# Linear attention and two feed-forward layers on one core: two attention units in one visit, a state kept twice, scores computed a visit ahead

## The chip, the cores and the metric

The kernel runs on one core of a Trainium2 chip. The metric is the device time of one execution, in microseconds (us). Five engines matter: TensorE (PE in the profile, its weight loads are PEld), VectorE (DVE), ScalarE (ACT), GpSimd (POOL), and SyncE (SP), which here does nothing but issue DMAs. Each engine runs its own instructions in the order of the program and waits on semaphores for the others.

## The reference: what is computed

A recurrent attention with a decay w for each feature and a bonus u, then two feed-forward layers. B = 4 batches, H = 8 heads, S = 768 tokens, D = 48.

```python
for t in range(S):
    cur = einsum('bhd,bhe->bhde', u[None] * k_t, v_t)
    y[:, :, t] = einsum('bhd,bhde->bhe', r_t, state + cur)
    state = w[None, :, :, None] * state + einsum('bhd,bhe->bhde', k_t, v_t)
x = y as (3072 tokens, 384)
h = x @ w_in;  g = max(h, 0) + alpha * min(h, 0);  x = g @ w_out       # first layer, 384 -> 2048 -> 384
h = x @ w_in2; g = h * tanh(softplus(h));          out = g @ w_out2    # second layer, same sizes
```

## The kernel before

The 768 tokens are cut into six blocks of 128 tokens; with four batches a block has 512 columns. **The first feed-forward layer** (stage A) is a row of 96 slots, one for each pair of a block and one of 16 hidden tiles of 128 features. A slot is nine TensorE matmuls of 128x512 into a PSUM tile `h` (`mA_h`, line 269: x and w are split into a high and a low part, which takes three passes), the activation on ScalarE and VectorE (`mA_g`: `m` on line 673, `g` on line 675), a split of g into `ghi` (`mA_hi`, line 187, ScalarE) and `glo` (`mA_lo`, line 190, VectorE), and nine matmuls into accumulators `acc` (`mA_out`, line 705), which run two slots later (`LAG`). Tile `h` has two buffers. **The second layer** (stage B) follows with 96 slots of its own and is not touched.

**The attention** feeds x to stage A block by block. It is worked in units. Units 0 to 3 are the first block, one batch each. From unit 4 on, a unit is a block j, a pair of batches bp and a half of 64 tokens (`seat_of_unit`): 4 units to a block, 24 in all. The order in a block before is pair 0 first half, pair 0 second half, pair 1 first half, pair 1 second half. A unit's small matmuls stand between two slots, after a slot's h matmuls and before its out matmuls: I call that a **visit**. `batch(u)` makes it: eight matmuls of the state with r for the other batch of the row group (`carried(False)`, line 534), the scores of unit u+1 (line 501), the products of k and v that update the state (line 550, `more_state`), the eight other carried matmuls (line 534), and masked scores times v (line 557). The profile shows each of these float32 matmuls as two records, 128 records to a full visit. The result stands in a `yt` bank and in one of the two buffers of `h`.

Around it, for each unit: the state T is multiplied in place by w to the 64th (`t_decay`, line 566 on ScalarE or 568 on VectorE; `other()` says which engine is free in a phase), the update is added (`t_update`, line 574, VectorE), `x_parts(u)` splits the result into the parts of x (ScalarE line 187, four operations with output y or x, then VectorE line 190, four). Since a head has 48 features, the last two heads fit into free rows of x, so x_parts of a second half also issues six DMAs on SyncE that move them there (line 639, `x<-y`). Ahead of a unit stand its loads (`load_unit`: r and k through line 301 for a pair's first half, `nat` through line 324), the scaling of r and k (`prep_pair`, line 419), the bonus terms (`prep_c`, `prep_c2`, `prep_kn`), the diagonal (`preset`, into tile `Ah`) and the mask (`masked`, line 505, VectorE, from the PSUM tile `sc` into `Ah`).

The order of all of this is a plan: `at(place, work)` puts a piece of work at a place counted in slots, a table `PLACES` overrides places of the first slots, and `run_plan` sorts by place. In `plan_unit(u, s)` the visit of unit u stands at s + 0.60, `t_decay` at s + 0.61, `x_parts` at s + 0.70, `t_update` at s + 1.25, and s comes from `AT`: every fourth slot from unit 6 on.

Of the kernel before, what the change touches and what calls it, by code (L numbers as in the profile page):

```python
# [31 lines left out]
C = 128  # L32
# [5 lines left out]
PR = 112  # L38
# [10 lines left out]
def seat_of_unit(u):  # L49

    j, r = divmod(u, 4)
    return j, r // 2, r % 2


def more_state(u):
# [10 lines left out]
    "pad_v 0": 8.499, "m_first 1": 8.549, "keep_warm 3##########": 8.599, "scores 0": 8.649, "dma_start": 8.699,  # L66
    "seats": 8.749, "masked 0": 8.799, "c_first 1": 8.849, "load_unit 3": 8.899, "prep_rk 1": 8.949,
    "load_unit 2": 8.999, "m_first 2": 9.049, "scale_Kn": 9.099, "more_raw 3": 9.149, "pad_v 1": 9.199,
# [20 lines left out]
    "mA_g 1": 14.049, "half_tables": 14.099, "states_first 0": 14.149, "w_hi (0,3)": 14.199, "w_lo (0,3)": 14.249,  # L89
# [74 lines left out]
def attention_and_two_ff(ctx: ExitStack, tc, rkT, nat, wT, ub, consts, w1, w2, alphaT, out):  # L164
# [353 lines left out]

    def batch(u):

        j, bp, half = seat_of_unit(u)
        pair, n, v = inp[u]
        A = A_t.pop(u)
        y = yt_t[u] = [bank("yt"), bank("h", 2)]
# [16 lines left out]
        if u + 1 < NU:  # L541
            scores(u + 1)
# [592 lines left out]
```

## Time and profile before

| | |
|---|---|
| device time, median of 3 runs | 860.72 us (860.19 to 861.66) |
| the profiled execution's own time, and its span | 860.91 us, 859.2 us |
| TensorE busy | 853.1 us, 99% of the span, granted clock full in every slice |
| VectorE, ScalarE, GpSimd busy | 629.2 us, 617.5 us, 109.3 us |
| chain that ended last | 95% of it is TensorE |

The span is the time between the first and the last instruction that the profiler recorded; the run's own time is 1.7 us longer. A busy TensorE counts a matmul from the start of its stream to its modelled end, so small matmuls that lie behind each other still show as busy.

### The profile page before, as it was taken

The numbers are of one execution on the slowest core, as the hardware profiler recorded it, in microseconds if no ns is written. First come the engines' busy times: TensorE is split into PE (matmuls) and PEld (weight loads), VectorE is DVE, ScalarE is ACT, GpSimd is POOL, SyncE is SP. The second block draws the span as 40 slices with busy tenths as digits, with TensorE's granted clock in tenths as the row PEclk, the third lists the DMA queues.
The fourth block names the chain that finished last, engine by engine and source line by source line (L and its number), as shares of the span: only waits on it lengthen the run. The fifth ranks groups of instructions, "written<-read, shape, count | busy, mean of one in ns | idle before, by whom it ended". The sixth has DMA issues, their size and how long they took to land.

```text
span 859.2 us, 16705 instructions
## 1 busy us (share of the span) xinstructions
PE 853.1 (99%) x6380; PEld 709.6 (83%) x6380; DVE 629.2 (73%) x974; ACT 617.5 (72%) x1205; POOL 109.3 (13%) x127
## 2 busy tenths in 40 slices
PE   9999999999999999999999999999999999999998
PEld 6888788888888888888888888888888888888897
DVE  8888666566656656554766878887887887887876
ACT  5989464445445445544656989989999998998886
POOL 3555441112211112100002000000000000000000
PEclk9999999999999999999999999999999999999999
DMA  9986644354255434213520200110110110100101
GB/s 335 283 260 176 184 144 130 90 194 137 86 161 167 145 98 158 65 65 134 161 87 6 111 1 2 32 43 1 29 46 1 28 47 0 28 11 1 26 12 37
DMA packets 65328, 79.95 MB, mean 93 GB/s; under 512 B 39648, under 2 KB 52448, under 8 KB 65248
## 3 DMA queue, kind: packets, MB, share of 16 engines
q1 hardware_dynamic: 64688, 78.78, 30.0%
q8 instruction: 50, 0.82, 0.4%
q14 instruction: 30, 0.25, 0.1%
q10 hardware_dynamic: 560, 0.10, 0.1%
HBM read 61.16 MB, written 15.73 MB: 89 GB/s over the span
## 4 chain that ended last, share of the span: by engine, by line
PE 95%; DMA 2%; ACT 2%; SPq 1%; DVE 0%; issue 0%; POOL 0%; ACTq 0%; DVEq 0%; POOLq 0%
PE h L269 45%; PE acc L705 22%; PE sc L835 8%; PE acc L835 8%; PE yt L835 4%; PE acc L833 3%; PE sc L501 1%; PE yt L833 1%; DMA w4r<-in_w 1%; PE h L534 1%; PE yt L557 1%; PE sc L550 1%; PE yt L534 1%; DMA w8u<-in_rkT 0%; SPq L639 0%
## 5 line engine op out<-in xcount | busy, mean ns | idle before, releaser
L269 PE MATMUL h<-x,w 128*128 128x512 f32 (+1 forms) x1746 | 415.3, 388 | 0.0
L269 PEld LDWEIGHTS h<-x,w 128*128 128x128 f32 x1746 | 325.3, 188 | 67.0 <-issue 0.4
L705 PE MATMUL acc<-ghi,w 128*128 128x512 f32 x516 | 174.9, 394 | 0.0
L673 ACT ACTIVATE m<-h 128x512 f32<-128x512 f32 x96 | 57.1, 595 | 91.1 <-PE h L269 90.9
L675 DVE SCALAR_TENSOR_TENSOR g<-m,oma,h 128x512 f32<-128x512 f32 x96 | 71.6, 746 | 60.7 <-ACT m L673 59.5
L705 PEld LDWEIGHTS acc<-ghi,w 128*128 128x128 f32 x516 | 96.9, 188 | 21.2
L187 ACT ACTIVATE ghi<-g 128x512 fp32r<-128x512 f32 x86 | 54.1, 630 | 68.9 <-PE acc L705 46.3
L705 PE MATMUL acc<-glo,w 128*128 128x512 f32 x258 | 100.5, 390 | 0.0
L190 DVE TENSOR_TENSOR glo<-g,ghi 128x512 fp32r<-128x512 f32 x86 | 62.4, 726 | 50.7 <-ACT ghi L187 50.2
L771 DVE SCALAR_TENSOR_TENSOR a<-ghi,h 128x512 f32<-128x512 f32 x96 | 66.0, 688 | 37.7 <-ACT ghi L768 31.2
L771 DVE SCALAR_TENSOR_TENSOR g<-s,c 128x512 f32<-128x512 f32 x95 | 66.6, 702 | 22.6 <-ACT s L768 21.0
L779 ACT ACTIVATE m<-h 128x512 f32<-128x512 f32 x96 | 56.4, 588 | 35.0 <-PE h L269 35.0
L190 DVE TENSOR_TENSOR gloB<-g,ghiB 128x512 fp32r<-128x512 f32 x105 | 72.1, 686 | 6.7 <-ACT ghiB L187 6.7
L768 ACT ACTIVATE ghi<-m,biases 128x512 f32<-128x512 f32 x96 | 69.6, 725 | 3.2
L187 ACT ACTIVATE ghiB<-g 128x512 fp32r<-128x512 f32 x105 | 64.8, 617 | 9.1 <-PE acc L705 5.5
L768 ACT ACTIVATE glo<-ghi,biases 128x512 f32<-128x512 f32 x96 | 68.1, 710 | 0.1
L768 ACT ACTIVATE s<-glo,biases 128x512 f32<-128x512 f32 x96 | 68.1, 709 | 0.0
L768 ACT ACTIVATE s<-s,biases 128x512 f32<-128x512 f32 x96 | 68.0, 708 | 0.0
L835 PE MATMUL sc<-ghiB,w 128*128 128x512 f32 x192 | 66.9, 389 | 0.0
L771 DVE SCALAR_TENSOR_TENSOR b<-ghi,a 128x512 f32<-128x512 f32 x96 | 65.7, 684 | 0.1
L771 DVE SCALAR_TENSOR_TENSOR c<-glo,b 128x512 f32<-128x512 f32 x95 | 65.7, 691 | 0.0
L835 PE MATMUL acc<-ghiB,w 128*128 128x512 f32 x192 | 61.7, 389 | 0.0
(200 smaller groups left out, 1149.9 us busy)
## 6 DMA issues: line engine op xcount, KB each, us to landing
wrawr<-in_w SPq DMA_DIRECT2D x28, 768.0 KB, 5.8
nat<-in_nat SPq DMA_DIRECT2D x40, 288.0 KB, 4.4
w2d<-wj SPq DMA_DIRECT2D x16, 384.0 KB, 2.6
wraw<-w2d SPq DMA_DIRECT2D x16, 384.0 KB, 3.0
rk<-in_rkT SPq DMA_DIRECT2D x40, 128.0 KB, 2.8
x2d<-xo SPq DMA_DIRECT2D x6, 768.0 KB, 3.8
x<-x2d SPq DMA_DIRECT2D x6, 768.0 KB, 4.4
rk<-in_rkT SPq DMA_DIRECT2D x40, 96.0 KB, 2.6
```

The lines of the kernel that those rows point to most:

```text
L187: act.activation(out=hi, in_=src, func=AF.Copy)
L190: eng.tensor_tensor(out=lo, in0=src, in1=hi.bitcast(F32), op=ALU.subtract)
L269: pe.matmul(h[:, n], w_in(layer, f, a, c), x[:, b, c, n], start=(k == 0), stop=(k == 3 * KC - 1))
L534: pe.matmul((y if same else over)[i][64 * q:64 * q + 64, p * HC:(p + 1) * HC], T[ROWS[h], 2 * bp + i, k, :], pair[i][ROWS[h], 0, k, t], st ...
L673: act.activation(out=m, in_=hA[s], func=AF.Relu, scale=-1.0)
L675: dve.scalar_tensor_tensor(out=g, in0=m, scalar=oma[:, f:f + 1], in1=hA.pop(s), op0=ALU.mult, op1=ALU.add)
L705: pe.matmul(acc[0][c], w_out(0, f, a)[:, c * 128:(c + 1) * 128], g[b], start=(f == 0 and k == 0), stop=(f == NF - 1 and k == 2))
L768: act.activation(out=out, in_=in_, func=AF.Square, scale=scale, bias=fin[bias])
L771: dve.scalar_tensor_tensor(out=out, in0=in0, scalar=scalar, in1=in1, op0=op0, op1=ALU.mult)
L779: act.activation(out=bnew("t", n), in_=v["h", n], func=AF.Tanh, scale=0.5)
L833: pe.matmul(acc[1][t][:, :DM], g[a][:, t * C:(t + 1) * C], w_out(1, f, b), **se)
L835: pe.matmul(acc[1][t], w_out(1, f, a)[:, t * 128:(t + 1) * 128], g[b], **se)
```

## The change: what it does

From block 2 on (the third), units 8 to 23, **two units share one visit**: `two(a)` handles units a and a+1, which are now both batch pairs of one half (`seat_of_unit` swaps the order for j of 2 or more). Eight visits stand at the slots of `AT2`, seven slots apart. Before the first of them a small visit of its own, `scores_of_two(8)`, computes the scores of units 8 and 9; from then on a visit ends with the scores of the next two units. The state has two tiles, T and Tn: `fade` on ScalarE writes the decayed state from the one to the other a good slot behind a visit, and in the next visit VectorE adds the products of k and v to it (line 722) as soon as the states matmuls are there; carried goes on reading the old tile. r and k of a block come in one load for all four batches (`load_seats`, line 438; r of odd blocks goes to a buffer of the weight staging), `prep_pair` works by r and k, and the last heads are moved by twelve DMAs of 16 rows for each two units instead of six for each pair of units (`last_heads`, line 826; for units 10 and 11 half of them are issued by ScalarE). Places of weight loads, scalings and of `mA_hi`/`mA_lo` in slots with a visit move; the first 81 slots' entries of `PLACES` are written anew. Units 4 to 7 still have visits of their own.

```diff
 def seat_of_unit(u):
     j, r = divmod(u, 4)
-    return j, r // 2, r % 2
+    return (j, r // 2, r % 2) if j < 2 else (j, r % 2, r // 2)
...
+    def scores_of_two(a):
+        so[a + 1] = NPR * HC
+        for u in (a, a + 1):
+            scores(u)
+
+    def fade(a):
+        now_T, next_T = T_of
+        for k in range(NPR):
+            act.activation(out=next_T[:, :, :, k, 0:D], in_=now_T[:, :, :, k, 0:D], func=AF.Copy, scale=w64[:, k:k + 1])
+
+    def two(a):
+        both, final = (a, a + 1), a + 2 == NU
+        y = yt_t[a] = yt_t[a + 1] = [bank("yt"), bank("h", 2)]
+        yo[a + 1] = NPR * HC
+        over = [sc_t[0][:, i] for i in range(2)] if final else y
+        for u in both:
+            carried(u, False, over, u == a, final and u > a)
+        if not final:
+            old, new_T = T_of
+            pool.memset(old[:, :, :, :, 63:64].rearrange("d b i k e -> d k i b e"), 0.0)
+            for n, u in enumerate(both):
+                states(u, n * D, 2)
+            for i in range(2):
+                t = new_T[:, :, i, :, 0:D].rearrange("d b k e -> d k b e")
+                dve.tensor_tensor(out=t, in0=t, in1=sc_t[0][0:PR, i, 0:2 * NPR * D].rearrange("d (k b e) -> d k b e", b=2, k=NPR),
+                                  op=ALU.add)
+        for u in both:
+            carried(u, True, y, final and u == a)
+        for u in both:
+            own(u, u == a + 1)
+        if not final:
+            T_of.reverse()
+            scores_of_two(a + 2)
...
+    def last_heads(u):
+        j, _, half = seat_of_unit(u)
+        x = x_t[j].bitcast(F32).rearrange("d i c (b t) -> d i c b t", b=B)[:, :, :, :, HALF[half]]
+        for q in range(2):
+            for c in range(KC):
+                for i in range(2):
+                    (act if i and u == 2 * B + 2 else dma).dma_start(out=x[48 + 64 * q:64 + 64 * q, i, c],
+                                  in_=y3_t[j][64 * q + 16 * c:64 * q + 16 * c + 16, i].bitcast(F32))
...
-    AT = {B: 2, B + 1: 5} | {u: 4 * u - 16 for u in range(B + 2, NU)}
+    AT = {B: 2, B + 1: 5, B + 2: 8, B + 3: 12}
+    AT2 = {8: (22, 1), 10: (29, 1), 12: (36, 0), 14: (43, 0), 16: (50, 0), 18: (57, 0), 20: (64, 0), 22: (71, 0)}
+    SHARED = {s for s, later in AT2.values() if not later}
...
+    def plan_two(a, s, later):
+        s += 0.14 * later
+        at(s + 0.56, two, a)
+        if a + 4 < NU:
+            at(s + 1.9, fade, a)
+        for u in (a, a + 1):
+            at(s + 0.6, x_parts, u)
...
+        at(17.8, scores_of_two, 2 * B)
...
-    "batch 4": 17.649, "mA_h 8": 17.699, "mA_g 7": 17.749, "w_scale (0,10)": 17.799, "w_join (0,10)": 17.849,
...
+    "prep_pair 17 0": 65.899, "two 14": 65.949, "x_parts 14": 65.999, "x_parts 15": 66.049, "prep_c 16": 66.099,
```

How the rows move on the engines. On TensorE, the middle of a visit before (unit 15, every full visit reads the same): `yt` and `h` are the two banks of the result, `sc` the PSUM tile of scores and states, `nat` holds k and v.

```order
L534 MATMUL yt<-rk,T 64x64
L501 MATMUL sc<-rk 64x64 x16
L550 MATMUL sc<-nat 48x48 x16
L534 MATMUL yt<-rk,T 64x64
L534 MATMUL h<-rk,T 64x64
```

The scores of the next unit stand in the middle of the visit, ahead of the states matmuls; the visit ends with masked scores times v, and the slot's out matmuls follow. The end of the visit of units 12 and 13 after the change, on TensorE (`Ah` the masked scores, `wrawq` r of an odd block, `acc` the accumulators of the slot's out matmuls):

```order
L680 MATMUL yt<-Ah,nat 48x64
L680 MATMUL h<-Ah,nat 48x64
L631 MATMUL sc<-wrawq,rk 64x64 x32
L892 MATMUL acc_2501<-ghi,w_424 128x512
L892 MATMUL acc_2501<-glo,w_424 128x512
```

The scores of both next units are now its last work, behind masked scores times v and ahead of the slot's out matmuls. On VectorE, around the visit of units 12 and 13, after the change (`Tn` and `T` are the two state tiles, `y_3129` the last heads):

```order
L320 SCALAR_TENSOR_TENSOR wj<-wrawr 128x768
L285 TENSOR_TENSOR glo<-g,ghi 128x512
L547 TENSOR_TENSOR rk<-rk,RKs 112x512
L547 TENSOR_TENSOR rk<-rk,RKs 112x512
L722 TENSOR_TENSOR T<-T,sc 112x4x2x48
L722 TENSOR_TENSOR T<-T,sc 112x4x2x48
L285 TENSOR_TENSOR y_3129<-yt,y_3129 112x64
L285 TENSOR_TENSOR y_3129<-h,y_3129 112x64
L285 TENSOR_TENSOR x<-yt,x 112x3x64
L285 TENSOR_TENSOR x<-h,x 112x3x64
```

Two additions to the state stand ahead of the splits of the result; before, an in-place decay (line 568) stood ahead of them and one addition (line 574) two operations behind. On SyncE, ahead of the copies of the last heads of units 4 and 5, before:

```order
L207 DMA wrawr<-in_w 128x1536 x2
L301 DMA rk<-in_rkT 64x2x256 x2
L301 DMA rk<-in_rkT 48x2x256 x2
L301 DMA rk<-in_rkT 64x2x256 x2
L301 DMA rk<-in_rkT 48x2x256 x2
L324 DMA nat<-in_nat 64x1152 x2
L639 DMA x<-y_905 16x2x256 x6
```

And after the change, at the same place:

```order
L302 DMA wrawr<-in_w 128x1536 x2
L438 DMA rk<-in_rkT 64x4x256 x2
L438 DMA rk<-in_rkT 48x4x256 x2
L421 DMA nat<-in_nat 64x1152 x2
L816 DMA x<-y_904 16x2x256 x6
```

Four loads of r and k stand ahead of the six copies where eight stood.

## Rows read from the trace of the kernel before

**Rows 1.** The page: busy time by engine, TensorE's granted clock, the chain by engine

```profile
PE 853.1 (99%) x6380; PEld 709.6 (83%) x6380; DVE 629.2 (73%) x974; ACT 617.5 (72%) x1205; POOL 109.3 (13%) x127
...
PEclk9999999999999999999999999999999999999999
...
PE 95%; DMA 2%; ACT 2%; SPq 1%; DVE 0%; issue 0%; POOL 0%; ACTq 0%; DVEq 0%; POOLq 0%
```

**Rows 2.** The waits of TensorE: us in total, times, longest

```profile
PE acc L656 <- POOL ghi L966: 1.3, 1, 1.3
PE h L534 <- DVE x L190: 0.8, 1, 0.8
PE sc L501 <- DVE A L505: 0.6, 1, 0.6
```

**Rows 3.** TensorE's timeline, one visit (unit 14): start, duration, engine, line, operation

```profile
205.87 2.20 PE L269 MATMUL h<-x,w 128*128 128x512 f32 x9
...
208.13 0.39 PE L705 MATMUL acc<-glo,w 128*128 128x512 f32 x1
...
209.95 2.20 PE L269 MATMUL h<-x,w 128*128 128x512 f32 x9
212.08 0.27 PE L534 MATMUL h<-rk,T 48*64 48x64 f32 x1
...
212.36 0.65 PE L501 MATMUL sc<-rk 48*64 48x64 f32 x32
212.83 0.54 PE L550 MATMUL sc<-nat 64*48 64x48 f32 x32
213.19 0.23 PE L534 MATMUL yt<-rk,T 48*64 48x64 f32 x1
...
213.43 0.22 PE L557 MATMUL yt<-Ah,nat 64*48 64x64 f32 x1
...
213.84 0.21 PE L557 MATMUL h<-Ah,nat 64*48 64x64 f32 x1
213.99 0.50 PE L705 MATMUL acc<-ghi,w 128*128 128x512 f32 x1
214.32 0.39 PE L705 MATMUL acc<-glo,w 128*128 128x512 f32 x1
```

**Rows 4.** TensorE's timeline, a later visit of the same kind (unit 20)

```profile
323.20 0.65 PE L501 MATMUL sc<-rk 48*64 48x64 f32 x32
...
325.17 0.39 PE L705 MATMUL acc<-glo,w 128*128 128x512 f32 x1
```

**Rows 5.** Timelines ahead of the visit of unit 7: ScalarE, and SyncE's issues

```profile
87.08 0.22 ACT L187 ACTIVATE y<-yt 112x64 fp32r<-112x64 f32 x1 [1.97 <-DMA x<-y]
...
72.99 5.87 SPq L301 DMA_DIRECT2D rk<-in_rkT  x8
...
80.66 4.88 SPq L639 DMA_DIRECT2D x<-y  x6
```

**Rows 6.** State lines by source line: ns min/median/max, first and last start

```profile
L574 DVE TENSOR_TENSOR T<-T,sc x18: 545/547/556, 70.4 to 365.1; 112x384 f32<-112x384 f32 x18
...
L568 DVE TENSOR_TENSOR T<-T,w x15: 550/1374/1406, 103.2 to 361.1; 112x384 f32<-112x384 f32 x15
...
L566 ACT ACTIVATE T<-T,w x12: 357/363/398, 59.7 to 84.7; 112x96 f32<-112x96 f32 x12
```

**Rows 7.** Timelines: the split of unit 7's result, TensorE, ScalarE, VectorE

```profile
90.55 0.22 PE L557 MATMUL h<-Ah,nat 64*48 64x64 f32 x1
...
90.81 0.22 ACT L187 ACTIVATE y<-yt 112x64 fp32r<-112x64 f32 x1 [1.22 <-PE h L557]
...
91.45 0.65 ACT L187 ACTIVATE ghi<-g 128x512 fp32r<-128x512 f32 x1
...
92.03 0.35 DVE L190 TENSOR_TENSOR x<-h,x 112x192 fp32r<-112x192 f32 x1
```

**Rows 8.** The page: the DMA queue that fetches TensorE's instructions

```profile
q8 instruction: 50, 0.82, 0.4%
```

More of the change, by code (lines that the diff above doesn't have):

```diff
@@ L317, in load_unit @@
         j, bp, half = seat_of_unit(u)
-        if half == 0:
-            rk_t[j, bp] = [att.tile([PR, 2, NPR, C], F32, tag="rk", name="rk", bufs=4) for _ in range(2)]
+        if half == 0 and u < 2 * B:
+            t = att.tile([PR, 2, 2, NPR, C], F32, tag="rk", name="rk", bufs=2)
+            rk_t[j, bp] = [t[:, i] for i in range(2)]
             for i in range(2):
@@ L324, in load_unit, with load_seats, rows_of @@
             dma.dma_start(out=n[HALF[i]], in_=nat[B * j + 2 * bp + i, HALF[half]])
-        inp[u] = (rk_t[j, bp], n, n[:, 2])
+        inp[u] = rk_t.get((j, bp)), n, n[:, 2]
+    def load_seats(u, n):
+        j, bp, _ = seat_of_unit(u)
+        if n == 0 and j % 2:
+            t = per.tile([128, 2 * DM, 2], U32, tag="wraw", name="wrawq", bufs=NRAW).rearrange("d n two -> d (n two)")
+            t = t[0:PR, 0:2 * NPR * C].bitcast(F32).rearrange("d (b p t) -> d b p t", b=2, p=NPR)
+            first, count = 2 * bp, 2
+            rk_t[j, n, bp] = t
+        else:
+            t = att.tile([PR, 2, 2, NPR, C], F32, tag="rk", name="rk", bufs=2).rearrange("d a b p t -> d (a b) p t")
+            first, count = 0, B
+            for k in range(2):
+                rk_t[j, n, k] = t[:, 2 * k:2 * k + 2]
+        for q, h, (a, b, o) in SEATED:
+            dma.dma_start(out=t[o:o + b - a, :, 2 * q:2 * q + 2].rearrange("d b p t -> d b (p t)"),
+                          in_=rkT[B * j + first:B * j + first + count, a:b, n, 2 * h:2 * h + 2].rearrange("b d p t -> d b (p t)"))
+    def rows_of(u, i, n):
+        j, bp, half = seat_of_unit(u)
+        if j < 2:
+            return inp[u][0][i][:, n, :, HALF[half]]
+        return rk_t[j, n, bp][:, i, :, HALF[half]]
+    yo = {}
+    so = {}
     RK = per.tile([PR, 2, NPR, C], F32, tag="w1", name="RK")
@@ L329, in attention_and_two_ff @@
     Kn = att.tile([128, 2, NPR, 2, D], F32, name="Kn")
-    T = att.tile([PR, B, NPR, 64], F32, name="T")
+    T_of = [att.tile([PR, NPR, 2, 2, 64], F32, name=name).rearrange("d k i b e -> d b i k e") for name in ("T", "Tn")]
+    T = T_of[0]
     def tables():
@@ L415, in prep_pair @@
     def prep_pair(u, i):
+        if u >= 2 * B:
+            j, bp, _ = seat_of_unit(u)
+            engine = pool if other() else dve
+            for b in range(2):
+                rk = rk_t[j, i, bp][:, b].rearrange("d p (h t) -> d p h t", h=2)
+                engine.tensor_tensor(out=rk, in0=rk, in1=RKs[:, i].unsqueeze(2).to_broadcast([PR, NPR, 2, HC]), op=ALU.mult)
+            return
+        w = RKs.rearrange("d i p t -> d (i p) t")
         rk = inp[u][0][i].rearrange("d i p (h t) -> d (i p) h t", h=2)
-        w = RKs.rearrange("d i p t -> d (i p) t")
         (pool if other() else dve).tensor_tensor(out=rk, in0=rk, in1=w.unsqueeze(2).to_broadcast([PR, 2 * NPR, 2, HC]), op=ALU.mult)
@@ L489, in scores @@
         sc = sc_t[0]
-        _, _, half = seat_of_unit(u)
         for j in range(NPR):
@@ L497, in scores @@
                     else:
-                        rk = inp[u][0][i]
-                        s = t = HALF[half]
-                        o = slice(j * HC, (j + 1) * HC)
+                        rk = rows_of(u, i, 0), rows_of(u, i, 1)
+                        o = slice(so.get(u, 0) + j * HC, so.get(u, 0) + (j + 1) * HC)
+                        pe.matmul(sc[HALF[i], h, o], rk[1][ROWS[h], j], rk[0][ROWS[h], j], start=True, stop=True)
+                        continue
                     pe.matmul(sc[HALF[i], h, o], rk[ROWS[h], 1, j, s], rk[ROWS[h], 0, j, t], start=True, stop=True)
@@ L517, in attend0 @@
                               start=(p == 3 and c == 0), stop=(p == 2))
[L519 to L524, printed above, removed]
-        t = HALF[half]
-        final = u == NU - 1
-        over = [sc_t[0][:, i] for i in range(2)] if final else y
-        def carried(same):
-            for r in range(2):
-                for h, q in ((0, 0), (1, 1), (0, 1), (1, 0)):
-                    i, k, p = (h if same else 1 - h), 2 * q + r, 2 * h + r
-                    pe.matmul((y if same else over)[i][64 * q:64 * q + 64, p * HC:(p + 1) * HC], T[ROWS[h], 2 * bp + i, k, :],
-                              pair[i][ROWS[h], 0, k, t], start=(r == 0 and (final or not same)),
-                              stop=(final and not same and r == 1))
-        carried(False)
-        if not final:
-            pool.memset(T[:, 2 * bp:2 * bp + 2, :, 63:64], 0.0)
-        if u + 1 < NU:
-            scores(u + 1)
-        if more_state(u):
-            st_t[u] = sc_t[0][:, :, NPR * HC:NPR * HC + NPR * D]
-            nf = n.rearrange("s i d -> s (i d)")
-            for k in range(NPR):
-                for i, h in ((0, 0), (1, 1), (0, 1), (1, 0)):
-                    p, q = HEAD[h, k]
-                    o = (2 * p + q) * D
-                    pe.matmul(st_t[u][ROWS[h], i, k * D:(k + 1) * D], nf[HALF[i], DM + o:DM + o + D], v[HALF[i], o:o + D],
-                              start=True, stop=True)
-        carried(True)
@@ new lines, in carried @@
+    def carried(u, same, banks, first=True, last=False):
+        bp, b, T = seat_of_unit(u)[1], yo.get(u, 0), T_of[0]
+        for r in range(2):
+            for h, q in ((0, 0), (1, 1), (0, 1), (1, 0)):
+                i, k, p = (h if same else 1 - h), 2 * q + r, 2 * h + r
+                pe.matmul(banks[i][64 * q:64 * q + 64, b + p * HC:b + (p + 1) * HC], T[ROWS[h], bp, i, k, :],
+                          rows_of(u, i, 0)[ROWS[h], k], start=(first and r == 0),
+                          stop=(last and r == 1))
@@ new lines, in states, with own @@
+    def states(u, o, wide=1):
+        _, n, v = inp[u]
+        st_t[u] = st = sc_t[0][:, :, o:]
+        nf = n.rearrange("s i d -> s (i d)")
+        for k in range(NPR):
+            for i, h in ((0, 0), (1, 1), (0, 1), (1, 0)):
+                p, q = HEAD[h, k]
+                e = (2 * p + q) * D
+                pe.matmul(st[ROWS[h], i, k * wide * D:(k * wide + 1) * D], nf[HALF[i], DM + e:DM + e + D], v[HALF[i], e:e + D],
+                          start=True, stop=True)
+    def own(u, last=True):
+        v, A, y, b = inp[u][2], A_t.pop(u), yt_t[u], yo.get(u, 0)
@@ L556, in batch @@
                 h, k = SEAT[p, q]
-                pe.matmul(y[i][ROWS[q], p * HC:(p + 1) * HC], v[HALF[i], o:o + D], A[HALF[i], h, k, :],
-                          start=False, stop=(p == PAIR[-1]))
+                pe.matmul(y[i][ROWS[q], b + p * HC:b + (p + 1) * HC], v[HALF[i], o:o + D], A[HALF[i], h, k, :],
+                          start=False, stop=(last and p == PAIR[-1]))
+    def batch(u):
+        y = yt_t[u] = [bank("yt"), bank("h", 2)]
+        carried(u, False, y)
+        bp = seat_of_unit(u)[1]
+        pool.memset(T[:, bp, :, :, 63:64], 0.0)
+        if u + 1 < 2 * B:
+            scores(u + 1)
+        states(u, NPR * HC)
+        carried(u, True, y, False)
+        own(u)
+    def scores_of_two(a):
[4 more added lines that the diff above has]
+        now_T, next_T = T_of
+        for k in range(NPR):
+            act.activation(out=next_T[:, :, :, k, 0:D], in_=now_T[:, :, :, k, 0:D], func=AF.Copy, scale=w64[:, k:k + 1])
[22 more added lines that the diff above has]
+            scores_of_two(a + 2)
     def t_decay(u):
         if more_state(u):
-            b = 2 * seat_of_unit(u)[1]
-            t = T[:, b:b + 2, :, 0:D]
+            t = T[:, seat_of_unit(u)[1], :, :, 0:D]
             if other():
@@ L613, in x_parts @@
         x = x_t[j].rearrange("d i c (b t) -> d i c b t", b=B)[:, :, :, 2 * bp:2 * bp + 2, HALF[half]]
-        if half == 0:
-            y3_t[j, bp] = att.tile([128, 2, 2, C], F32R, tag="y3", name="y3", bufs=1)
-        y3 = y3_t[j, bp]
-        if u == NU - 1:
+        pair = u >= 2 * B
+        if pair:
+            if bp == 0:
+                y3_t[j] = att.tile([128, 2, B, HC], F32R, tag="y3", name="y3", bufs=1)
+            y3 = y3_t[j][:, :, 2 * bp:2 * bp + 2]
+        else:
+            if half == 0:
+                y3_t[j, bp] = att.tile([128, 2, 2, C], F32R, tag="y3", name="y3", bufs=1)
+            y3 = y3_t[j, bp][:, :, :, HALF[half]]
+        y = [y[i][0:PR, b:b + NPR * HC] for i in range(2)]
+        if u + 2 >= NU:
             total = att.tile([128, 2, NPR, HC], F32, tag="Ah", name="Ah", bufs=2).rearrange("s i p t -> s i (p t)")
@@ L626, in x_parts @@
                                       op=ALU.add)
-            y = [total[:, i] for i in range(2)]
-        parts = [(y3[0:PR, 0, i, HALF[half]], y3[0:PR, 1, i, HALF[half]], y[i][0:PR, 3 * HC:4 * HC]) for i in range(2)]
-        parts += [(x[0:PR, 0, :, i], x[0:PR, 1, :, i], y[i][0:PR, 0:3 * HC].rearrange("d (c t) -> d c t", c=KC))
+            y = [total[0:PR, i] for i in range(2)]
+        parts = [(y3[0:PR, 0, i], y3[0:PR, 1, i], y[i][:, 3 * HC:4 * HC]) for i in range(2)]
+        parts += [(x[0:PR, 0, :, i], x[0:PR, 1, :, i], y[i][:, 0:3 * HC].rearrange("d (c t) -> d c t", c=KC))
                   for i in range(2)]
@@ L634, in x_parts @@
             lo_of(dve, lo, hi, t)
-        if half == 1:
+        if not pair and half == 1:
             x = x_t[j].bitcast(F32)[:, :, :, 2 * bp * C:2 * (bp + 1) * C]
@@ L905, in at @@
         named.add(key)
-        place = PLACES.get(key, place)
+        place = PLACES.get(key, max(place, 13.6))
         if place is not None:
@@ L957, in plan_unit, with plan_prep @@
             at(n + K["c2"], prep_c2, u + 2)
+    def plan_two(a, s, later):
[5 more added lines that the diff above has]
+            at(s + 0.6, x_parts, u)
+        for u, d in ((a + 3, 0.601), (a + 4, 3.71)):
+            if u < NU:
+                at(s + d, load_unit, u)
+        late = seat_of_unit(a)[2]
+        at(s + (0.605 if late else 0.625), last_heads, a)
+        if not late and a + 4 < NU:
+            odd = (a // 4 + 1) % 2
+            at(s + 0.62, load_seats, a + 4, 1)
+            for n in range(2 if odd else 1):
+                at(s + 2.4, load_seats, a + 4 + n, 0)
+            for n in range(2):
+                at(s + 3.1 + n, prep_pair, a + 4 + n, 1)
+                at(s + 5.1 + n, prep_pair, a + 4 + n, 0)
+    def plan_prep(a, n):
+        late = 0.6 * (a == 2 * B)
+        for k, u in enumerate((a, a + 1)):
+            at(n - 5.9 + k, prep_c, u)
+            at(n - 4.35 + 0.5 * k + late, prep_c2, u)
+            at(n - 4.3 + k, prep_kn, u)
+            at(n - 4.3 + 0.6 * k + late, preset, u, 0)
+            at(n - 3.9 + 0.3 * k + late, preset, u, 1)
+            at(n - (2.2, 1.2)[k] if a > 2 * B else n - (0.95, 0.8)[k], masked, u)
     with tc.manual_schedule():
```

70 lines of the change are left out of this document (43 added, 27 removed), and 275 rows, old and new, of the table PLACES.

## The prediction

> **What bounds the kernel now.** I read the page first: TensorE is busy for 853.1 of 859.2 us, its granted clock stands at full in every slice, and 95% of the chain that ended last is TensorE [rows 1]. The list of TensorE's waits comes next. It has three entries in the whole span, 1.3, 0.8 and 0.6 us [rows 2]. So the time is the sum of what TensorE issues, and a change can win in two ways only: fewer or closer instructions on TensorE, or the end of one of these waits. Every new wait adds in full. The timeline of a visit gives the prices [rows 3]. A slot without a visit has its h matmuls at 205.87 and the second out matmul at 208.13, 2.26 us, which is ten matmuls of 0.226. With a visit the same two marks are 209.95 and 214.32, 4.37 us. One unit costs TensorE 2.11 us. A later visit repeats it: from the first score to the second out matmul 1.97 us at 323.20 [rows 4], 1.96 at 212.36 [rows 3].
>
> The visit falls into parts, by the starts in [rows 3]. The ninth h matmul starts at 209.95 + 8 x 0.226 = 211.76, so **entry** (large tiles to small) is 0.32. The first carried group takes 0.28, the scores 0.47, the states 0.36, the second carried group 0.24, masked scores times v 213.43 to 213.84, 0.41. **Exit** to the first out matmul is 0.15, and from there to the second 0.33. The sum is 2.56; less two ordinary matmul steps (0.45) it is the 2.11.
>
> **The change, part by part.** *Two units in one visit.* No matmul goes away or is added. What goes is one entry, one exit and one slow first out matmul for each pair. A two-unit visit is 0.32 + 0.28 + 3 x 0.24 + 2 x 0.36 + 2 x 0.41 + 2 x 0.47 + 0.15 + 0.33 - 0.45 = 3.83 us, against 2 x 2.11 = 4.22. Before, units 8 to 23 cost 14 full visits, one without states (1.75, unit 21) and one without states and scores (1.28, unit 23): 32.57 us. After, there are seven full two-unit visits (26.81), the last without scores and states (3.83 - 0.94 - 0.72 = 2.17) and the separate visit for the first two scores (0.32 + 0.94 + 0.15 + 0.33 - 0.45 = 1.29), while unit 7's visit loses the scores of unit 8 (0.47). That is 29.80 us: **-2.8 us**.
>
> *The wait of 0.8 us.* It stands in the visit of unit 7 [rows 2]: the bank `h` is not free until VectorE has split the result of unit 6. ScalarE had stood for 1.97 us until 87.08, since the tile y that it writes was still being copied [rows 5]. The copies were issued from 80.66 on, behind eight loads of r and k that took SyncE 5.87 us, 0.73 each [rows 5]. After the change four larger loads stand there, so the copies can start up to 2.9 us earlier, more than the 1.97 that ScalarE waited. I take the whole **-0.8 us**; the other bound is 0, if it is the result of unit 5 and not the queue that is late.
>
> *The decay.* `fade` is four operations on ScalarE of twice the elements of the old decay, which took 0.36 each [rows 6]. By the rows of larger splits it would be some 0.4 to 0.5 each, 2 us for each visit, seven times. It has seven slots (28 us) to hide in, and ScalarE is idle for 28% of the span [rows 1]: nothing, as long as nothing urgent stands behind it. In exchange VectorE loses the in-place decay.
>
> *The additions.* This is a new wait. The next two units' scores overwrite the tile that holds the states, so they wait until VectorE has read them in two additions. Behind the scores stand all of TensorE's work, the out matmuls of the slot first. The cover is the second carried groups (2 x 0.24) and masked scores times v (2 x 0.41), 1.30 us. An addition that reads one operand from PSUM took 0.545 to 0.556 us in all 18 cases [rows 6]; two make 1.10. With hand-over some 0.1 to 0.2 us remain: **0**, on the edge. The other end is the row of the in-place decay of the same shape, 1.37 in the median [rows 6]: 2.75 us, 1.45 more than the cover, in each of seven visits. I take the addition's row, since it has the same operands and the same operation.
>
> *The split of two units.* Eight operations on ScalarE and eight on VectorE now follow a visit, and the bank `h` comes free at their end. For one unit ScalarE starts 0.26 us after the start of the last matmul, takes 0.64, and VectorE ends its last part at 92.38, 1.83 us after that matmul [rows 7]. A second unit adds 0.64 on ScalarE and about as much behind it: 2.5 to 2.8 us, and up to 3.4 if one `ghi` of 0.65 or a slot's g goes first. What covers it until the next h matmuls that need the bank is scores (0.94), exit and first out (0.48) and eight more out matmuls (1.8): 3.2 us. So between 0 and 0.2 us in the visits where h follows after one row of out matmuls, which are two or three: **+0.4**.
>
> *Copies, loads and places.* Each visit issues twelve small DMAs at SyncE, where six took 4.88 us [rows 5], 0.81 each: some 9.8 us at worst for a visit against seven slots. They hurt where a block's first slot follows soon: blocks 3 and 5, and the half of units 10 and 11 that ScalarE issues stands ahead of an m in its queue. Bounds are 0 and the whole second half of the copies, 4.9 us, once; a weight scaling that waits for a raw load can hold `fade` and the m behind it by up to 0.6. The rows of before show SyncE with no wait on TensorE behind it other than the one above, so I stay near the low end: **+0.6**.
>
> *The instruction stream.* TensorE's 6380 records took 50 fetches [rows 1, 8], one for every 128 records, and a fetch is 0.4% of 16 x 859 us over 50, 1.1 us. A visit of one unit is 128 records in 2.1 us and shows no gap; one of two units takes two fetches in 3.8 us, 1.9 apart. As long as one fetch of 1.1 us has time while the other block runs, this is **0**; if it did not, I bound it by the part of a fetch that sticks out, 0.3 us for each of eight visits. [...]
>
> **The sum.** 860.9 (the profiled execution's own time) - 2.8 - 0.8 + 0.4 + 0.6 = 858.3 us. That execution lies 0.2 above the median of the runs shown, so I forecast **858.1 us**, 0.3% less.
>
> **The rivals.** (1) *The additions run like the decay*: VectorE's rows of the same shape split into 0.55 and 1.37 [rows 6], and the new tile's layout (four by two by 48) is one that no row shows. Then TensorE stands 1.45 us in each of seven visits, +10.1 us: 868 us. It decides against the change from 0.5 us for a visit on (3.5 us in all). Against it: all 18 rows with a PSUM operand are fast, and the slow ones have both operands in SBUF. (2) *The waits only move*: splits, copies and late loads at block starts cost 3 to 4 us in place of 1, as the 0.8 us of unit 7 came from one late queue [rows 5]. This gives 860 to 861.5 us. Against it: seven slots lie between visits, and each wait would show once or twice only. (3) *The fetches stick out*: 0.3 us for each of eight visits, 2.4 us: 860.5 us. For it: the records come twice as dense for twice as long as ever before; against it: no gap at any place of a one-unit visit [rows 3, 4].
>
> **Chances and range.** Forecast, with its waits between 0 and 2 us (857 to 859): 0.55. Rival 2: 0.22. Rival 3: 0.12. Rival 1 or another lasting wait: 0.11. A measurement of this kernel can tell about 0.2%, 1.7 us, from no change. Nearly all of the forecast is faster by that (0.54), and of rival 2 and 3 a third (0.09); another 0.21 of them falls within it; rival 1 and the worst of rival 2 are slower (0.16). The range takes the forecast's low end with the waits at nothing and the last 0.6 us of other waits gone, 856.6, and reaches up to rival 2's far end, 862.
>
> **What would show it.** Right: records of a two-unit visit with one entry of 0.32 us and one exit, 3.8 us for the visit; TensorE's busy time about 3 us smaller, with no wait of the line of scores (631) on VectorE's line 722; no wait of 0.8 us in the visit of unit 7. Wrong: a wait of line 631 of 1 us or more in each visit, with line 722 at 1.3 us instead of 0.55 (rival 1); waits of line 364 (h) on lines 282 or 285 or on `x<-y`, at 36, 43 and the block starts (rival 2); gaps in the middle of the small matmuls with no releaser named, the same in each visit (rival 3). A fall of more than 4 us would mean that I missed something that TensorE no longer does.

## The result and the profile after

The changed kernel takes 869.18 us in the median of six runs (867.05 to 871.02), the kernel before 860.65 beside it: ratio 1.0095, interval 1.0077 to 1.0113. It is slower by 8 us where I forecast 2.6 less, and its runs spread over 4 us where those of before spread over 1.5. The profiled execution is the fastest of the six, 867.05.

The page after: busy time by engine, and the chain by engine.

```profile
PE 853.6 (99%) x6380; PEld 710.7 (82%) x6380; DVE 610.1 (71%) x954; ACT 630.9 (73%) x1336; POOL 141.2 (16%) x149
...
PE 95%; DMA 2%; ACT 1%; issue 1%; DVE 1%; SPq 0%; ACTq 0%; DVEq 0%
```

The page hides the loss. TensorE's busy time, which I had said would fall by about 3 us, rose by 0.5; matmuls that ran at half clock (0.50 for 3.3 us, below) are in it, and I do not account for the rest. "Issue" in the chain went from 0% to 1%. The waits of TensorE answer to [rows 2].

```profile
PE acc L892 <- ACT ghi L282: 3.2, 1, 3.2
PE acc L892 <- issue: 1.5, 1, 1.5
PE h L364 <- issue: 1.3, 1, 1.3
PE acc L843 <- POOL ghi L1188: 1.3, 1, 1.3
PE yt L680 <- issue: 0.4, 1, 0.4
PE sc L633 <- DVE A L637: 0.3, 1, 0.3
PE h L364 <- DVE x L285: 0.2, 1, 0.2
```

The 0.8 us on VectorE's x of before is gone. One wait of 3.2 us on ScalarE has come, and three on "issue", that is on nothing that a semaphore shows.

**The visits came out as computed.** TensorE's timeline, the visit of units 12 and 13, answers to [rows 3].

```profile
190.90 2.20 PE L364 MATMUL h<-x,w 128*128 128x512 f32 x9
...
193.03 0.27 PE L657 MATMUL h<-wrawq,T 48*64 48x64 f32 x1
...
193.54 0.90 PE L670 MATMUL sc<-nat 64*48 64x48 f32 x64
...
196.68 0.50 PE L892 MATMUL acc<-ghi,w 128*128 128x512 f32 x1
197.02 0.39 PE L892 MATMUL acc<-glo,w 128*128 128x512 f32 x1
```

From the start of the h matmuls (190.90) to the start of the second out matmul (197.02) it is 6.12 us; less the 2.26 of a slot without a visit, 3.86 (forecast 3.83). The additions to the state, by source line, answer to [rows 6].

```profile
L722 DVE TENSOR_TENSOR Tn<-Tn,sc x8: 547/550/555, 129.2 to 332.3; 112x384 f32<-112x384 f32 x8
L722 DVE TENSOR_TENSOR T<-T,sc x6: 547/551/555, 162.4 to 294.6; 112x384 f32<-112x384 f32 x6
```

All fourteen took 0.55 us and no scores waited for them. The queue ahead of unit 7, on SyncE and ScalarE, answers to [rows 5].

```profile
72.76 2.95 SPq L438 DMA_DIRECT2D rk<-in_rkT  x4
...
77.07 4.56 SPq L816 DMA_DIRECT2D x<-y  x6
...
85.04 0.23 ACT L282 ACTIVATE y<-yt 112x64 fp32r<-112x64 f32 x1 [0.17 <-DMA x<-y]
```

The copies start 3.6 us earlier and ScalarE waits 0.17 in place of 1.97.

**Loss one, 5.2 us near slot 60.** The rows are of SyncE's issues, ScalarE, VectorE and TensorE.

```profile
299.79 13.62 SPq L302 DMA_DIRECT2D wrawr<-in_w  x2
313.46 7.70 SPq L826 DMA_DIRECT2D x<-y  x12
...
310.43 0.58 ACT L860 ACTIVATE m<-h 128x512 f32<-128x512 f32 x1
318.00 0.88 ACT L311 ACTIVATE wrawr<-wrawr 128x768 f32<-128x768 f32 x1 [7.00 <-DMA wrawr<-in_w]
...
319.55 0.61 ACT L282 ACTIVATE ghi<-g 128x512 fp32r<-128x512 f32 x1
...
311.70 1.31 DVE L320 SCALAR_TENSOR_TENSOR wj<-wrawr 128x768 uint32<-128x768 uint32 x1
...
320.21 0.80 PE L892 MATMUL acc<-ghi,w 128*128 128x512 f32 x1 [3.18 <-ACT ghi L282]
```

SyncE issues a raw weight load (tile 11) and stands at the next (tile 12) until 313: weight staging has three buffers, two hold r of block 5, and the third comes free when VectorE has joined tile 11, at 313.0. The load lands at 318. ScalarE has its scaling next in line and stands for 7.0 us, a ghi behind it, and TensorE behind that ghi. What follows is in the windows (busy us and instructions of PE, PEld, DVE, ACT, POOL; then the granted clock).

```profile
316.70:320.20 3.50, 0.33 (x2) 0.00 (x0) 0.01 (x1) 2.20 (x4) 0.00 (x0) 1.00 0.19 41
320.20:324.10 3.90, 3.89 (x9) 2.81 (x10) 3.14 (x5) 2.96 (x8) 0.62 (x1) 0.56 0.51 162
```

After the stand TensorE runs at half clock (0.50 from 320.2 to 323.5 us) for most of 3.9 us, with steps of 0.43 us where 0.227 is normal: 3.35 us of wait and 1.87 of clock, 5.2 in all.

**Loss two, 3.8 us with no releaser.** TensorE's timeline behind the visits of units 10 and 16.

```profile
164.55 2.35 PE L364 MATMUL h<-x,w 128*128 128x512 f32 x9
168.42 0.40 PE L892 MATMUL acc<-ghi,w 128*128 128x512 f32 x1 [1.52 <-issue]
...
264.50 1.30 PE L364 MATMUL h<-x,w 128*128 128x512 f32 x5
267.13 1.09 PE L364 MATMUL h<-x,w 128*128 128x512 f32 x4 [1.33 <-issue]
```

The steps from one matmul to the next are 1.69 and 1.49 us too long there, and 0.60 inside the visit of units 8 and 9. The DMA queues tell what is late. Two windows of the visit of units 10 and 11 (161.0 to 165.6 us, the first row; 165.7 to 167.1, the second and third) and one of units 12 and 13 (195.7 to 196.7, the last row). The columns are queue and kind, packets, MB, and the time of the packets as a share of 16 engines' time; a packet counts whole in the window in which it starts, so a share can pass 100%.

```profile
q1 hardware_dynamic: 297, 1.24, 78.8%
...
q1 hardware_dynamic: 91, 0.33, 103.5%
q8 instruction: 1, 0.02, 5.5%
...
q8 instruction: 1, 0.02, 5.9%
```

In the first row 1.24 MB of weights and nat are moved, and no fetch. In the next two the fetch comes, beside more data. In the last, in the quiet visit, there is the fetch and no other packet. The trace has the start and the landing of each fetch. The table has the second fetch of each visit, in us from the visit's first small matmul, the DMA share from about the visit's start to that fetch, and the gap behind the visit:

| visit of units | 10 | 12 | 14 | 16 | 18 | 20 |
|---|---|---|---|---|---|---|
| second fetch starts | 4.95 | 2.71 | 3.51 | 5.83 | 2.56 | 2.58 |
| DMA share up to it | 0.77 | 0.02 | 0.79 | 0.95 | 0.00 | 0.00 |
| gap behind the visit | 1.69 | none | none | 1.49 | none | none |

At 12 there is 0.32 on VectorE's x, no fetch. At 14 the loads are as dense as at 10, but the fetch starts 1.4 us sooner and no gap follows. The gap inside the visit of units 8 and 9 has its load ahead of it: from 124 to 127.84 us the data queue moved 1.18 MB (a share of 90.5%), and the visit's first fetch started at 127.84, 0.1 us into the visit, where at units 12 to 20 the first fetch starts 0.7 to 1.5 us ahead of the visit. And each gap of this kind, here and in all runs below, ends 1.3 to 1.7 us after a fetch has landed; three of the change with a named releaser (those that end at 20.66, 199.18 and 320.21 us) end 4.2, 2.5 and 15.8 us after the last landing. **The sum**: 860.9 - 2.8 - 0.8 + 5.2 + 3.8 + 0.4 (splits, at units 12 and 14) = 866.7, measured 867.05 in the profiled execution.

### The profile page after: what moved, and what is told of

Same layout as the page of the kernel before. It is cut to its first block, busy times and chain, and to the rows that moved or that the text cites. A ratio compares the mean times of both kernels' runs of the same rounds, so it can differ in the third digit from the quotient of the medians.

```text
span 865.3 us, 16871 instructions
## 1 busy us (share of the span) xinstructions
PE 853.6 (99%) x6380; PEld 710.7 (82%) x6380; DVE 610.1 (71%) x954; ACT 630.9 (73%) x1336; POOL 141.2 (16%) x149
## 4 chain that ended last, share of the span: by engine, by line
PE 95%; DMA 2%; ACT 1%; issue 1%; DVE 1%; SPq 0%; ACTq 0%; DVEq 0%
PE h L364 45%; PE acc L892 22%; PE sc L1022 8%; PE acc L1022 8%; PE yt L1022 4%; PE acc L1020 3%; PE sc L631 1%; PE yt L1020 1%; DMA w4r<-in_w 1%; PE yt L680 1%; PE sc L670 1%; PE h L657 1%; PE yt L657 1%; DMA wrawr<-in_w 1%; DMA w8u<-in_rkT 0%
## 5 line engine op out<-in xcount | busy, mean ns | idle before, releaser
L285 DVE TENSOR_TENSOR glo<-g,ghi 128x512 fp32r<-128x512 f32 x86 | 68.1, 792 | 63.7 <-ACT ghi L282 63.3
```

Of the source, the lines that this page charges most:

```text
L285: eng.tensor_tensor(out=lo, in0=src, in1=hi.bitcast(F32), op=ALU.subtract)
```

## The experiments

For each loss theories stood against each other. For loss one: the order of the queue (mine), or a lack of buffers that only moves the wait. For loss two: fetches queue behind bulk DMAs and the denser visits no longer hide it (mine); or dense visits alone outrun the fetch; or bulk DMAs slow TensorE directly.

**e0_again**, no edit. 

> The changed kernel as it is, profiled a second time. If the gaps of 1.3 to 1.7 us with no releaser behind a visit are fetches of instructions that queue behind bulk DMAs, they come again in the visits of units 8, 10 and 16 or in that of 14, with other sizes (0 to 3 us each), while the wait of 3.2 us on ScalarE's ghi near slot 60 and the half clock behind it come again at the same place within 0.5 us. If the gaps are a fixed price of the order of the small matmuls, they come again at the same places with the same sizes within 0.1 us.

869.11 us in a single run. Gaps again at units 8 (0.41), 10 (1.50) and 16 (0.98), each 1.3 to 1.5 us behind a landing, and one of 2.2 us at 82.49 in the visit of unit 6, which had none in the first profile. The wait near slot 60 is 3.8 us, 0.6 more than before, where I had allowed 0.5. Places repeat, sizes do not: a fixed price is out.

**e1_raw12.**

```diff
-"w_scale (1,12)": 74.199   -"w_join (1,12)": 74.399   -"w2_store 12": 74.449
+"w_scale (1,12)": 75.16    +"w_join (1,12)": 75.17    +"w2_store 12": 75.18
```

> Only the scaling, joining and storing of weight tile 12 of the second layer are moved, some two slots later. Theory: ScalarE stood 7.0 us for that raw load with a ghi behind it; TensorE's wait of 3.2 us and the 1.9 us at half clock behind it go, so the time falls by about 5 us, from 869 to 864. Rival: the raw load is late for lack of a buffer, the wait only moves to the next thing behind the scaling: the time stays within 1 us of 869.

871.04 us (ratio 1.0115, 1.0098 to 1.0132): the wait only moved, as the rival had it, though it had put the time within 1 us of 869. The new first row of TensorE's waits:

```profile
PE yt L657 <- POOL T L717: 3.6, 1, 3.6
```

And SyncE's timeline:

```profile
302.86 13.78 SPq L302 DMA_DIRECT2D wrawr<-in_w  x2
```

ScalarE no longer stands, but SyncE still does, for 13.8 us, and nat of unit 22 is behind the load in its queue; GpSimd waits 11.89 us for nat with the memset of the state behind it, and the next visit for the memset. Behind that wait the granted clock was 0.51 from 332 to 339 us.

**e2_quiet** and **e3_both**. The loads in the visits of units 10, 14 and 16 go behind the copies of the last heads, with the scalings later; e3 adds the edit of e1.

```diff
-"load_raw 1 4": 59.499   -"load_unit 13": 59.999   -"w_scale (1,4)": 60.499
+"load_raw 1 4": 60.056   +"load_unit 13": 60.054   +"w_scale (1,4)": 61.14
...
-"load_raw 1 7": 65.699   -"load_unit 17": 66.499   -"w_scale (1,7)": 66.149   -"w_join (1,7)": 66.199   -"w2_store 7": 67.099
+"load_raw 1 7": 66.562   +"load_unit 17": 66.555   +"w_scale (1,7)": 67.62    +"w_join (1,7)": 67.63    +"w2_store 7": 67.64
...
-"load_raw 1 9": 69.649   -"load_unit 19": 69.849   -"load_seats 20 1": 69.899   -"w_scale (1,9)": 69.699   -"w_join (1,9)": 69.799
+"load_raw 1 9": 69.962   +"load_unit 19": 69.955   +"load_seats 20 1": 69.97    +"w_scale (1,9)": 71.36    +"w_join (1,9)": 71.37
```

> Only loads are moved: those of weights, of nat and of r and k that were issued during the visits of units 10, 14 and 16 go behind the copies of the last heads, and the weight scalings that need them later. Theory: a fetch of instructions starts about 1 us after its request when the DMA queues are quiet and 2 to 4 us after it when bulk loads are under way, so the gaps behind the visits of units 10 and 16 (1.7 and 1.5 us) go and the median falls by 3 to 4 us, to 865 or 866. Rival: two visits' worth of small matmuls outrun the fetch whatever the DMAs do: the gaps stay and the time stays at 869.

> Both moves at once. By the theory the two add up: 869 - 5 - 3.5 = 860 to 861, and the profiled execution has only small gaps left (0.6 us in the visit of units 8 and 9). If the predicted gain of 3.6 us by the visits themselves is real, it can come out as low as 858.5. Rival (gaps belong to dense visits): 864.

885.62 us (ratio 1.0293, 1.0272 to 1.0314) and 890.37 (1.0329, 1.0285 to 1.0373). Both theories missed: the loads came too late for what needs them. TensorE's waits of e2, the first two rows:

```profile
PE h L364 <- DVE g L862: 5.5, 3, 4.0
PE h L680 <- issue: 2.9, 2, 1.6
```

With so many new waits the times decide nothing. The starts of the fetches do say something: in the visits of units 10 and 14, whose loads had been moved away, the second fetch started 2.62 and 2.80 us into the visit (e3: 2.48 and 2.80), as in the quiet visits, where without the edit it is 3.8 to 5.0 and 3.4 to 4.0, and the gap behind units 10 is gone. Gaps of "issue" came instead at units 16 and 18, inside the visits.

**e4_order.** The order that e1 called for: tile 11 joined at once, the raw load of tile 12 behind the last heads and nat.

```diff
-"w_join (1,11)": 73.949   -"load_raw 1 12": 73.099
+"w_join (1,11)": 73.47    +"load_raw 1 12": 74.06
-"w_scale (1,12)": 74.199   -"w_join (1,12)": 74.399   -"w2_store 12": 74.449
+"w_scale (1,12)": 75.16    +"w_join (1,12)": 75.17    +"w2_store 12": 75.18
```

> Only around weight tile 12 of the second layer: tile 11 is joined as soon as it is scaled, the raw load of tile 12 is issued behind the last heads and nat of unit 22 in place of ahead of them, its scaling two slots later. Theory: the loss near slot 60 comes from SyncE, which stood 13.6 us at the raw load for want of a buffer (two of three hold r of block 5) with everything else behind it; issued in this order nothing stands, so the wait of 3.2 to 3.8 us and the half clock behind it go and no wait on GpSimd's memset takes their place: 869.1 - 5 = 864. Rival: any order only moves the wait, as in the run before: 868 to 871.

861.5 us in ten runs beside 861.78 of before: ratio 0.9999, 0.999 to 1.0008. SyncE's issues and ScalarE's scaling of tile 12:

```profile
300.67 0.37 SPq L302 DMA_DIRECT2D wrawr<-in_w  x1
301.79 8.09 SPq L826 DMA_DIRECT2D x<-y  x12
...
311.87 0.54 SPq L302 DMA_DIRECT2D wrawr<-in_w  x1
...
319.45 0.89 ACT L311 ACTIVATE wrawr<-wrawr 128x768 f32<-128x768 f32 x1
```

Nothing stands, and neither the wait on ghi nor one on the memset is left: the same three buffers do in this order, so the rival is out. The edit is worth 0.96%, 8 us by the medians, where the two profiles of the change showed 5.2 and some 6 for this wait (see the end of the next section).

**e5_split** and **e6_order_split**. The scores of the next units get a visit of their own one slot or two later; e6 adds the order of e4.

```diff
             T_of.reverse()
-            scores_of_two(a + 2)
+            if a not in (8, 10, 12, 14, 16, 18, 20):
+                scores_of_two(a + 2)
...
+    "scores_of_two 10": 57.24, "scores_of_two 12": 60.44, "scores_of_two 14": 63.24, "scores_of_two 16": 66.69,
+    "scores_of_two 18": 69.74, "scores_of_two 20": 73.19, "scores_of_two 22": 76.19,
...
```

> The scores of the next two units become a visit of their own, one slot or two behind their visit, so no visit has more than 192 records; loads stay where they are. Theory (a fetch must be usable before the small matmuls have used up the block before, some 2 us apart in a dense visit): the gaps of 1 to 1.7 us with no releaser at the visits of units 8, 10 and 16 go, 2.9 to 3.8 us in all, and seven entries and exits come back at 0.39 us, 2.7: 868, within 1 us of the change. Rival (the gaps come from bulk loads alone, whatever TensorE does at the time): the gaps stay, 869.1 + 2.7 = 872.

> The last two edits together: 864 by their sum (869.1 - 5 - 3.5 + 2.7 = 863.5), and the spread from run to run falls below that of the change (4 us), as no long visit is left. Rival: the spread stays.

877.21 us (ratio 1.0177, 1.016 to 1.0193) and 870.27 (1.0103, 1.0086 to 1.012). TensorE's waits of e6, the first three rows:

```profile
PE h L680 <- issue: 2.7, 2, 2.0
PE h L364 <- DVE x L285: 2.0, 2, 1.1
PE h L364 <- DMA x<-y: 1.6, 1, 1.6
```

Without the scores the visit is 0.93 us shorter, so the h matmuls that need its bank come before the split is done (the cover of 3.2 us that I had counted with them). And gaps of 2.2 and 0.95 us now stand inside the visits of units 10 and 14. I read this so: the length of a visit is not the only thing; where in it the 128 records of a fetch end is another. As a test between the theories this one is inconclusive. Only the smaller spread of e6 came as expected (1.4 us over four runs).

**e7_dense.** The scores of the next units are computed five times in three quiet visits.

```diff
-            scores_of_two(a + 2)
+            for _ in range(5 if a in (12, 18, 20) else 1):
+                scores_of_two(a + 2)
```

> The dense stretch by itself: in the visits of units 12, 18 and 20, which had no bulk load under way and no gap, the scores of the next two units are computed five times in place of once, 256 records more in each of these three visits. Without gaps this costs 4 x 0.94 = 3.8 us a visit. If a fetch takes about 3.4 us from its request until it can be used even with quiet DMAs (1.0 to its start, 1.0 to land, 1.4 to the end of a gap), each further 128 records, worth 2.0 us, bring a gap of 1 to 1.4 us: two gaps, 2 to 3 us in each visit. If only bulk loads delay the fetches, there is no gap of over 0.3 us in them.

897.52 us in a single run. TensorE in the visit of units 12:

```profile
195.32 1.34 PE L631 MATMUL sc<-wrawq,rk 48*64 48x64 f32 x79
198.61 3.14 PE L631 MATMUL sc<-wrawq,rk 48*64 48x64 f32 x128 [1.95 <-issue]
203.71 3.26 PE L631 MATMUL sc<-wrawq,rk 48*64 48x64 f32 x112 [1.96 <-issue]
```

Two gaps in each of the three visits, 10.6 us of "issue" in all, and 128 records from one to the next. They are 1.4 to 2.3 us long, some longer than I expected. Behind the first gap the granted clock fell (0.61 from 198.6 to 201.8 us, 0.50 from there to 207), so the two rows of 128 and 112 took longer than at full clock; TensorE outran the fetch even so. The fetch that ends the first gap of each visit started at 195.72, 305.50 and 352.61 us, and no packet of the data queue was under way in the windows just ahead (194 to 196, 304 to 306, 350 to 352.6); behind the second there were loads of nat as well. So in these visits a fetch did not keep up with these matmuls for longer than a visit even where no load stood ahead of it. I read this so: the visits of the change sit at the edge of what is hidden, and bulk loads push some of them over it.

**e8_quiet16**, on top of e4.

```diff
-"load_unit 19": 69.849   -"load_seats 20 1": 69.899
+"load_unit 19": 69.955   +"load_seats 20 1": 69.96
```

> On top of the order around weight tile 12, two loads are moved: nat of unit 19 and k of block 5, which were issued during the visit of units 16 and 17, are issued behind the copies of the last heads. Theory: the fetch for the end of that visit then starts some 2 us earlier, the gap of 2.2 us behind it shrinks to below 0.6: about 1.8 us less than with the order alone, 0.2% under the kernel before. Rival (the gap belongs to the visit): the gap stays at 2 us and the time with it.

862.14 us in ten runs beside 861.17 (ratio 1.0009, 0.9994 to 1.0025). The gap behind the visit of units 16 was 0.82 us where e4 had 2.16, as its second fetch started 5.44 us into the visit and not 6.46. That is not shown to be the edit: six profiles with the loads where they were have starts of 5.26 to 6.46. They do show that the gap goes with the start: 0.76 us at 5.26 (e7), 0.98 at 5.50 (e0), 1.49 at 5.83 (the change), 1.46 at 5.89 (e1), 1.99 at 6.25 (e9), 2.16 at 6.46 (e4). What the edit did do: a gap of 0.78 us appeared inside the visit of units 18, whose first fetch now started 0.27 behind the visit's start where it had been 0.87 ahead, as the loads behind the moved ones ran later (DMA share 0.95 to 1.08 from 286 to 290 us, where e4 has 0.27 and less from 288 on). No net gain.

**e9_bulk**, on top of e4, and **e10_bulk_before**, on the kernel before. Twelve stores that nothing reads.

```diff
     def masked(u):
...
+        if u in (19, 21):
+            for k in range(12):
+                dma.dma_start(out=dose_d[k], in_=A_t[u].rearrange("s q p t -> s (q p t)"))
```

In e10 the units are 14, 16 and 18.

> On top of the order around weight tile 12, twelve stores of 262 KB each to a scratch buffer in DRAM, which no one reads, are issued just ahead of the visits of units 18 and 20, which had no bulk load under way and no gap. Theory: the second fetch of each of these two visits starts 3 us or more after its request in place of 0.9 to 1.2, and a gap of 1.5 us or more with no releaser appears behind each, ending 1.3 to 1.5 us after the fetch has landed. Rival (the bulk loads have nothing to do with it): no gap there, as before.

> The kernel before with the same twelve stores issued just ahead of the visits of units 14, 16 and 18. Theory: the fetches there start late as well, 2 to 6 us after the request, but the next block of instructions is 10 us or more away behind a visit of one unit: no gap on TensorE, the time within 2 us of 861, unless a later load runs late. Rival (bulk transfers slow TensorE by themselves): gaps of 1 us and more at these three visits, 864 to 867.

e9 took 871.81 us in a single run, e10 861.77. In e9 the visit of units 18 has its first fetch at +0.32 us (-0.87 in e4) and a gap of 0.71 in its middle, its second at +5.28 (2.85) and no gap behind it: with the visit itself 0.7 later that fetch came just in time. The second batch of stores missed its visit: SyncE issued it at 339.69 us, behind the visit of units 20 (334.86 to 338.4), whose second fetch started at 2.54 with no gap. So one visit was tested, and its gap came in half the size that I expected, at the place that the fetch explains. In e9, SyncE's issues and ScalarE, then the first two rows of TensorE's waits:

```profile
290.62 7.17 SPq L642 DMA_DIRECT2D dose<-Ah  x12
...
298.33 0.57 SPq L303 DMA_DIRECT2D wrawr<-in_w  x1
...
339.69 9.12 SPq L642 DMA_DIRECT2D dose<-Ah  x12
...
306.44 0.88 ACT L312 ACTIVATE wrawr<-wrawr 128x768 f32<-128x768 f32 x1 [6.06 <-DMA wrawr<-in_w]
...
PE h L365 <- DVE x L286: 4.1, 1, 4.1
PE h L365 <- issue: 1.8, 1, 1.8
```

And all of them in e10:

```profile
PE acc L660 <- POOL ghi L970: 1.3, 1, 1.3
PE h L538 <- DVE x L191: 1.1, 1, 1.1
PE sc L502 <- DVE A L506: 0.3, 1, 0.3
```

The 4.1 us are the load of weight tile 11, queued behind my stores: ScalarE stood 6.06 us for it with a split of the visit's result behind it. The 1.8 is the gap at units 16, where nothing was added. In e10 no wait on issue appears at all, though the fetches started 2.86, 4.43 and 2.88 us into the visits of units 14, 16 and 18 where it had been 2.13, 2.94 and 1.73. These bulk transfers did not slow TensorE by themselves, and the one-unit visits stood a fetch that was 0.7 to 1.5 us late.

## Why the prediction was wrong

**Visits, -2.8: right.** 3.86 us measured where 3.83 was computed. **The wait of unit 7, -0.8: right**; the copies came earlier by more than ScalarE had waited. Both are shown by the trace of the change, not by an edit of their own. **The additions, 0: right**, and rival 1 fell with them: fourteen at 0.55 us. **The decay, 0: right** in itself, 0.44 us an operation. **The split of two units, +0.4: right** in the sum, 0.32 and 0.11 at units 12 and 14, though I had allowed 0.2 for one visit.

**"Copies, loads and places", +0.6, was mis-sized: it measured 5.2 us and more.** I had the last link of its mechanism, a weight scaling that waits for a raw load and holds what is behind it, and bounded it by 0.6 and, for the copies, 4.9. I looked at block starts and did not ask how many staging buffers were left once r of an odd block lives in two of three. That is not in the trace of before, where nothing of the kind happens; it is in the diff (the buffer of `load_seats`), and the order of SyncE's queue shows the second raw load ahead of everything else. The clock's fall behind the wait, 1.87 us, was no part of my sum. Shown: e1 took the wait off ScalarE and it came back through SyncE's queue and GpSimd; e4, which frees the queue, gives 8 us back by the medians.

**"The instruction stream", 0, is the step that failed in kind.** I took the fetch to be the 1.1 us that its packet takes, against 1.9 between fetches, and bounded it at 0.3 a visit. The time that counts was more than the packet's: 1.3 to 1.7 us pass from the landing to the end of a gap in every case, and behind bulk loads the second fetch started 4.95 and 5.83 us into the visit (units 10 and 16), 2.3 and 3.2 us later than in the quiet visits. The total was 3.8 us in the profile, in three places, not 0.3 in eight. Rival 3 had the mechanism and not the size. The 0.3 us was an estimate of mine that no row gave. For long bursts of small matmuls the runs show this: in e7 a gap of 1.4 to 2.3 us came for each further 128 records, the first in each visit with no load ahead of its fetch; in the kernel before, with 50 fetches, and at the quiet visits of the change (units 12, 18 and 20) TensorE has no wait on "issue".

So the gain of 3.6 us shows in the trace and was given back twice: 5 to 8 us by one order in SyncE's queue, some 3 us by fetches. With the first mended (e4) the change is even with the kernel before, and the gaps left in its profile (0.43, 0.33 and 2.16 us at units 8, 10 and 16) are about as large as the forecast gain.

**Open.** By the medians e4 gave 2 to 3 us more than the profiles charge to its wait. The profiles themselves agree: the change's is the fastest of its six, e4's the slowest of its ten, and their first visits begin at different times (that of unit 4 at 56.77 and 58.53 us; before, 57.02). From there to the end of the span the change takes 808.53 us, e4 802.37 and the kernel before 802.18: 6.2 us for the edit, the 5.2 of the wait and 0.9 of smaller gaps. e0, whose 869.11 us is at the median of the change, takes 810.97; the 2.4 more are mostly its gap of 2 us at unit 6. That gap stands in three of the eleven profiles made from the change (e0, e1, e9) and is a late fetch too: the one that started at 73.9 to 75.5 us in the other eight started at 81.4 to 82.2 in these, and in e0 the DMA share from 74 to 80 us was 0.86 to 1.14. Why it went ahead of those loads in some runs and not in others is not shown, and e9 has the gap with the new order, so e4's edit does not cure it. I have no version that beats the kernel before: e4 and e8 are even with it.

## What to carry to other kernels

Merging bursts of small matmuls saved an entry and an exit each time here (3.86 us for a visit of two units, 2 x 2.11 for two of one), but it doubled the records in one go from 128 to 256, and where the second fetch started late (4.95 and 5.83 us into the visit) gaps of 1.69 and 1.49 us stood behind it: ask where a fetch's 128 records end inside the burst, and what the DMA queues carry at that moment. When a tile moves into a pool of staging buffers, count what is left and find the next DMA that needs one: SyncE stood 13.62 us at such a load, with twelve copies and nat behind it in its queue. The engine that stood at the end was not the one to mend: with the wait taken off ScalarE (e1) the time was 871.04 us, with the queue in another order (e4) 861.5.

## What the runs showed of the hardware

- TensorE's fetches (50 of 16 KB for 6380 matmul records, one to about 128) started later when bulk loads were under way (in the change a DMA share of 0.77 to 0.95 up to the fetch, 0.00 to 0.02 in the quiet visits): the second fetch of a visit started, in the change, e0 and e4, 2.6 to 3.1 us into the quiet visits of units 12, 18 and 20 and 3.4 to 6.5 into those of units 10, 14 and 16, but 2.5 to 2.8 at units 10 and 14 once their loads had been moved away (e2, e3). TensorE, where it stood, went on 1.3 to 1.7 us after the landing.
- In a stretch of 320 records of matmuls of 64 columns at the end of a visit TensorE stood once for each 128 records, 1.4 to 2.2 us the first time, with no data packet just ahead of the fetch (e7).
- After a stand of 3.2 us the granted clock was 0.56 over the next 3.9 us (0.50 for the first 3.3), and the matmuls there took 1.9 us longer (the change).
